# Another written-out order for the first long convolution and the front behind it

## The chip, the cores and the metric

The kernel runs on one core of one Trainium2 chip. The metric is the device time of one execution in microseconds (us). The engines are named as in the profile: TensorE (PE, with its weight loads as PEld), VectorE (DVE), ScalarE (ACT), GpSimd (POOL) and SyncE (SP), whose queue issues nearly all transfers.

## The reference

Four layers act on one sequence x of 2048 rows and 512 columns, each on a layer-normalized copy and with a residual sum: a local attention (A), a long convolution (B), and both again with the same weights.

```python
x = x + _A_ref(_layernorm(x), A_wqkv, A_wo)
x = x + _B_ref(_layernorm(x), B_A_re, ..., B_Dskip)
x = x + _A_ref(_layernorm(x), A_wqkv, A_wo)
x = x + _B_ref(_layernorm(x), B_A_re, ..., B_Dskip)
```

`_A_ref` has 32 heads of 16; each row attends to 8 rows at distances 0, 2, ..., 14 behind it. `_B_ref` makes a kernel K of 2048 taps for each column from the state-space parameters, and convolves each column with it by Fourier transforms of length 4096:

```python
Kf = rfft(pad(K)); Uf = rfft(pad(u))
y = irfft(Uf * Kf)[:L] + u * Dskip
```

## The kernel before

**Stages.** The program makes K, runs the first attention, then the first convolution, the second attention and the second convolution. The stage of this case is the first convolution (`FftB` with `tag` 0) with the *front* of the second attention behind it: layer norm, transposes and the projections to keys and queries.

**The convolution.** The transforms are matrix products in two steps. The columns are split into two groups of 256, and each kind of step below is done 16 times: numbers 0 to 7 are group 0, numbers 8 to 15 group 1. Each step is some matmuls into a result tile in PSUM, and a copy out of it (`evac`, L758, by ScalarE or VectorE) unless something else is said.

- `K`: first step of the transform of K (16 matmuls, L769, from `k_perm`).
- `U`: the same for the normalized input u, which lies in the tile `xnT`.
- `k`: second step for K (16 matmuls, L776). Its copy is a spectrum `kn`. It needs all eight `K` of its group.
- `u`: second step for u (L776). Its copy `ub` (L835) is always ScalarE's. It needs all eight `U` of its group. There are three `ub` buffers.
- `m`: the product. VectorE multiplies `ub` by `kn` and by `ks`, a copy of the spectrum with its rows swapped pairwise (two multiplies, L822), into the tile `t`.
- `y`: first inverse step (32 matmuls, L849), into `z`. It needs all eight `m` of its group. Group 0's `z` overwrites `xnT`.
- `z`: second inverse step, over four of the 16 row blocks; `z01` is group 0, rows 4 to 7. It needs all eight `y` of its group. With ScalarE, TensorE adds x (L873) and ScalarE copies the sum into `x_sb` (L880); with VectorE, VectorE adds (L878).

In what follows a letter with a number from 0 to 15 names a step (m15 is the last product); in the order strings the number is left out, because each kind is counted through.

**Transfers.** All of them are in SyncE's queue, in the order of the program. Behind a `k`, `kf_load` (L804) issues the two transfers of its swap `ks`, as soon as there is a buffer (`pump`, L794). Behind an `m`, `kf_dram` gets the spectrum for the second convolution (L825, the *store*), and the product's two buffers are free for later `k` and swaps. When all that is done, the queue goes on with the weights of the second attention (`front_w`, L244 and L245).

**Result tiles.** Four PSUM tiles are used in turn (`ptile`, L753), so a step waits for the copy four steps before it. The step `S` (`front_pools`, L1417) gives two of them to the front.

**The order.** `fb.run` (L882) reads one token after the other and issues the instructions of each. Inside `manual_schedule` each of TensorE, VectorE, ScalarE and SyncE works through its instructions in exactly that order. In a token a last `A` means ScalarE, `D` VectorE. `ORDER0` (L50) is the convolution, `ORDERF` (L56) goes on with it and mixes the front in. `LATE0` names small steps of the layer norm of u that are issued behind the first seven `K`; the first `U` waits for the normalized rows that one of them writes on GpSimd (L189).

**The front's tokens.** `h` row statistics of one group (four `bn_stats`, L142, VectorE), `a` their sum-up (L1424), `p` the reciprocal deviation (two small steps of ScalarE), `n` the normalized rows (L189, VectorE), `T` sixteen transposes into two PSUM tiles (L261), `E` the copy out of one of the two (L263), `P` a projection to keys (four matmuls, L272, copied by ScalarE, L275), `Q` one to queries (L215), `x` shifted copies of keys (L285). A first digit is the block of 512 rows, except in `h` and `z`, where it is the group, and in `Q`, where it is the block of queries.

```python
for tok in order.split():
    op, ix = tok[0], [int(c) for c in tok[1:] if c.isdigit()]
    eng = dict(A="act", D="dve", B="both").get(tok[-1])
    ...
    n = cnt[op] = cnt.get(op, -1) + 1
    g, t = divmod(n, 8)
```

Of the kernel before, what the change touches and what calls it, by code (L numbers as in the profile page):

```python
# [21 lines left out]
S = 2048  # L22
# [25 lines left out]
zktkKkUEETkeUUktKTkkUkKTUUeKkkpkxpKUxkpUEUxUKkqUxUUUUpqoUkpoxKXUQxoUkpkKXZpxXxpxZZ  # L48
"""
ORDER0 = """  # L50
KD KA KA KD KA KA KD KA KD KA KD kA kA KD kA KD UA UD UA UD UA kD UA UD UA KD
kA kD u kD kA u UA m KD m u u UD UA UA UA m UD u m KA UD u m u kA kD m kA UA
kD u kA m kA kD u m u kA m m u u yD yA u m yA u m m m u u m m
"""
LATE0 = "a s t g r b m"
ORDERF = """  # L56
yA yA yA yA yA yA yD yA yA yA z01D yD yA yA z00A z10A z11A h01 h00 h10 a0 z12A
p0 h11 z02A n0 a1 z03A h02 S T0 p1 E01D n1 E00A h12 a2 z13A P02 P01 h03 T1
E10A Q00 E11D p2 P03 P00 n2 h13 P10 P12 a3 T2 E21D E20A p3 n3 P11 P13 P23 P21
T3 E31D x1 E30A P20 P22  # L60
"""
ORDER1 = """
UD UA UD UA UD UA UD UA UD UA UD u UD u u m UA u m UD UA m u m u m
# [1440 lines left out]
```

## Time and profile before

| what | value |
|---|---|
| median of 3 runs (413.72 to 416.47) | 414.1 us |
| the profiled execution | 415.31 us, of which the span of instructions is 413.5 us |
| mean granted TensorE clock | 0.993 |
| TensorE busy | 323.4 us (78%) |
| VectorE busy | 382.7 us (93%) |
| ScalarE busy | 324.6 us (79%) |
| GpSimd busy | 37.3 us (9%) |
| first matmul of the convolution, first copy by VectorE | 193.28, 193.96 us |
| last product m15 ended | 242.55 us |
| first transposes of the front | 257.09 us |
| first product of the second attention (L332) | 275.72 us |

All times in the rows are microseconds from the start of the span. Shares are means over stages with different limits, so a stage is read by itself. In an answer, `[1.71 <-DMA w_sb<-kf_sb]` behind an instruction says that its engine stood idle for 1.71 us before it, and that this transfer ended the wait. `x4` is a run of four like instructions, with the time from the first's start to the last's end. The names of tiles can be those of the memory that they share: `w_sb`, `kn`, `kf_sb` and `kf_nat` are all spectra and swaps here.

### The profile page before, as it was taken

Reading aid. Unit: us, or ns where it says so; the run is one execution under the profiler, and the core shown is the slowest. Engines: PE = TensorE matmul, PEld = TensorE weight load, DVE = VectorE, ACT = ScalarE, POOL = GpSimd, SP = SyncE. Lnnn points to the kernel's source line nnn. Section 1 sums busy time; section 2 is a strip of 40 time slices with the busy share of each in tenths; the row PEclk is TensorE's granted clock in tenths of the full one; section 3 lists DMA queues with packets and bytes.
Section 4 is the critical chain, followed back from the end, with each engine's and each line's share of the span. In section 5 each row is a group of like instructions: output and inputs, shape, how many; then the busy total and the mean of one; then the engine's idle time right before and its main releaser. Section 6 shows DMA issues by size and latency. Waiting matters only on the chain.

```text
span 413.5 us, 15577 instructions
## 1 busy us (share of the span) xinstructions
PE 323.4 (78%) x6929; PEld 225.1 (54%) x6929; DVE 382.7 (93%) x500; ACT 324.6 (79%) x557; POOL 37.3 (9%) x48
## 2 busy tenths in 40 slices
PE   2000169899999988889998769999999979997775
PEld 2000126657756655556887658653466655566664
DVE  7999999999799999997999949979889999989985
ACT  5999999896445579997999988874566658889962
POOL 3000200000396000000400000000000020000000
PEclk9999999999999999999999989999999999999998
DMA  7930832123014756393235586750043018504507
GB/s 215 403 107 13 88 77 71 33 55 77 15 44 111 195 175 190 85 395 122 79 118 194 184 292 171 257 177 0 2 115 91 3 53 360 157 3 141 170 4 204
DMA packets 62325, 54.22 MB, mean 131 GB/s; under 512 B 33869, under 2 KB 50738, under 8 KB 60978
## 3 DMA queue, kind: packets, MB, share of 16 engines
q1 hardware_dynamic: 62250, 53.22, 42.0%
q8 instruction: 54, 0.88, 0.9%
q14 instruction: 13, 0.11, 0.1%
q10 hardware_dynamic: 8, 0.00, 0.0%
HBM read 30.15 MB, written 13.24 MB: 105 GB/s over the span
## 4 chain that ended last, share of the span: by engine, by line
PE 40%; DVE 21%; ACT 7%; DMA 6%; issue 5%; SPq 5%; DVEq 0%; ACTq 0%
DVE pav L457 7%; PE pq L388 6%; PE pk L1195 5%; PE pp L1133 4%; DVE a1s L758 4%; PE pq L215 3%; PE L L344 3%; DVE prod L332 3%; PE pp L272 3%; SPq L1300 2%; DMA w_sb<-w_dram 2%; PE po L472 2%; PE pb L849 2%; PE pq L483 2%; DVE t L822 2%
## 5 line engine op out<-in xcount | busy, mean ns | idle before, releaser
L457 DVE TENSOR_TENSOR pav<-attn,v_ext 128x4096 bf16<-128x4096 bf16 (+1 forms) x34 | 72.9, 2155 | 0.0
L332 DVE TENSOR_TENSOR prod<-qT,kT_ext 128x4096 bf16<-128x4096 bf16 x29 | 65.9, 2297 | 3.6 <-PE L L344 3.2
L472 PE MATMUL po<-ident,pav 64*128 64x64 bf16 x2048 | 36.0, 190 | 13.7 <-DVE pav L457 7.9
L472 PEld LDWEIGHTS <-pav 64*128 64x128 bf16 x2048 | 32.4, 95 | 24.8 <-DVE pav L457 17.1
L1123 PE MATMUL pt<-ident,x_blk 128*128 128x128 bf16 x64 | 6.3, 241 | 42.2 <-DMA w_dram<-w_q 40.7
L1037 DVE TENSOR_TENSOR A_t<-A_t,pow_t 128x1024 bf16<-128x1024 bf16 (+4 forms) x46 | 38.0, 868 | 0.2
L835 ACT CAST ub<-pb 128x1024 bf16<-128x1024 f32 x32 | 32.1, 1042 | 1.2 <-ACT a1s L758 0.3
L776 PE MATMUL pb<-a1s,w_sb 128*128 128x64 bf16 x768 | 27.5, 193 | 6.9 <-ACT a1s L758 2.6
L483 PE MATMUL pq<-wop,oT 128*128 128x512 bf16 x128 | 32.8, 379 | 0.0
L390 ACT CAST v_ext<-pq 128x512 bf16<-128x512 f32 x32 | 18.8, 587 | 17.0 <-PE pq L388 15.7
L1133 PE MATMUL pp<-xnT,kT_ext 128*128 128x512 bf16 x96 | 26.8, 407 | 5.4 <-ACT qT L1138 2.5
L388 PE MATMUL pq<-wv,xnT 128*128 128x512 bf16 x128 | 30.8, 379 | 0.0
L758 DVE CAST a1s<-pb 128x1024 bf16<-128x1024 f32 x23 | 27.0, 1214 | 3.4 <-PE pb L769 3.4
L776 PEld LDWEIGHTS <-w_sb 128*128 128x128 bf16 x768 | 25.0, 98 | 9.4 <-issue 7.5
L1123 PEld LDWEIGHTS <-x_blk 128*128 128x128 bf16 x64 | 4.8, 107 | 44.6 <-ACT x_blk L187 43.2
L758 ACT CAST a1s<-pb 128x1024 bf16<-128x1024 f32 x25 | 24.9, 1037 | 2.2 <-PE pb L769 1.9
L474 ACT CAST oT<-po 128x512 bf16<-128x512 f32 x32 | 18.5, 578 | 9.7 <-PE po L472 9.5
L849 PE MATMUL pb<-Wp,t 64*128 64x64 bf16 x512 | 19.6, 195 | 6.4 <-ACT ub L835 1.8
L849 PEld LDWEIGHTS <-t 64*128 64x128 bf16 x1024 | 17.8, 98 | 11.2 <-issue 6.3
L1195 PEld LDWEIGHTS <-A_t 128*64 128x64 bf16 (+1 forms) x512 | 21.8, 103 | 3.7 <-issue 0.2
L1195 PE MATMUL pk<-B_t,A_t 128*64 128x84 bf16 (+1 forms) x512 | 23.6, 201 | 0.0
L215 PE MATMUL pq<-xnT,kT_ext 128*128 128x512 bf16 x96 | 23.5, 379 | 0.0
(241 smaller groups left out, 823.1 us busy)
## 6 DMA issues: line engine op xcount, KB each, us to landing
w_sb<-w_dram SPq DMA_DIRECT2D x8, 1024.0 KB, 7.1
w_dram<-xnT SPq DMA_DIRECT2D x1, 4096.0 KB
kf_ring<-kf_dram SPq DMA_DIRECT2D x13, 256.0 KB, 4.5
kf_ring<-kf_dram SPq DMA_DIRECT2D x26, 128.0 KB, 3.7
v_ext<-v_ext SPq DMA_DIRECT2D x4, 784.0 KB, 6.1
x_blk<-in_A_x_dram SPq DMA_DIRECT2D x4, 512.0 KB, 4.0
kT_ext<-in_A_wqkv_dram SPq DMA_DIRECT2D x4, 512.0 KB, 9.5
x_sb<-in_A_x_dram SPq DMA_DIRECT2D x4, 512.0 KB, 5.7
```

Source lines behind the costliest of these rows:

```text
L215: nc.tensor.matmul(pq[:], lhsT=self.wqk[:, dt, ft * P:(ft + 1) * P], rhs=self.xnT[:, dt, q * 512:(q + 1) * 512], start=(dt == 0), stop=(dt ...
L332: nc.vector.tensor_tensor(pr, self.qT[q][:, ft].unsqueeze(1).to_broadcast([P, W, 4, P]), kap, ALU.mult)
L388: nc.tensor.matmul(pp[:], lhsT=xnT[:, dt, a * P:(a + 1) * P], rhs=wv[:, dt, :], start=(dt == 0), stop=(dt == NDT - 1))
L457: nc.vector.tensor_tensor(pv[:, i], attn[:, n % 4].unsqueeze(2).to_broadcast([P, W, DH // parts, H]), vap, ALU.mult)
L472: nc.tensor.matmul(po[:, h, 0, i * nt + ft, :], lhsT=pvf[rows, i, w, ft * P:(ft + 1) * P], rhs=ident[rows, rows], start=(w == 0 and ft + i ...
L483: nc.tensor.matmul(pw[:], lhsT=oT[:, ftp, :], rhs=self.wo[:, ftp, :], start=False, stop=(ftp == NDT - 1))
L758: (self.nc.scalar.copy if eng == "act" else self.nc.vector.tensor_copy)(dst, src)
L776: nc.tensor.matmul(p2[:, j, :], lhsT=self.w2[:, ec * EC + j, :], rhs=a1s[:, ec * EC + j, :], start=True, stop=True)
L849: nc.tensor.matmul(p3[:, h, j, :], lhsT=tt[rows, dql, :], rhs=w[rows].rearrange("p m d -> p (m d)"), start=first, stop=not first)
L1037: return lambda: nc.vector.tensor_tensor(*args)
L1133: nc.tensor.matmul(pps[kind, b, ft][:], lhsT=la.wqk[:, dt, c:c + P], rhs=la.xnT[:, dt, b * 512:(b + 1) * 512], start=(dt == 0), stop=(dt = ...
L1195: nc.tensor.matmul(o, lhsT=lhs, rhs=Bt[:, ri, c * CH + ql].rearrange("p b g -> p (b g)"), start=(not half and j % 4 == 0 and ri == 0), sto ...
```

## The change

Two order strings are replaced. Each kind of step occurs as often as before, and nothing else is edited. Some copies go to the other engine: in the convolution VectorE has eight `K` instead of nine, five `U` instead of six, seven `k` instead of six and five `y` instead of three; in the front E20 and E30 go from ScalarE to VectorE.

```diff
 ORDER0 = """
-KD KA KA KD KA KA KD KA KD KA KD kA kA KD kA KD UA UD UA UD UA kD UA UD UA KD
-kA kD u kD kA u UA m KD m u u UD UA UA UA m UD u m KA UD u m u kA kD m kA UA
-kD u kA m kA kD u m u kA m m u u yD yA u m yA u m m m u u m m
+KD KA KA KA KA KD KD KA KA KD kA kD kA KD KA KD UA kD UA UA UD UA UD UA KD UA kA kD kA u kD UA u UA m KD m u UD m u UA u m KA u UD kA UA m UD kD m kA UA u u m u kD u kA kD kA u kA m u u u m m m u m m yA m yD yA u yA yA m m yA yD yA yD yA yD yA z01D yA
 """
 LATE0 = "a s t g r b m"
 ORDERF = """
-yA yA yA yA yA yA yD yA yA yA z01D yD yA yA z00A z10A z11A h01 h00 h10 a0 z12A
-p0 h11 z02A n0 a1 z03A h02 S T0 p1 E01D n1 E00A h12 a2 z13A P02 P01 h03 T1
-E10A Q00 E11D p2 P03 P00 n2 h13 P10 P12 a3 T2 E21D E20A p3 n3 P11 P13 P23 P21
-T3 E31D x1 E30A P20 P22
+yA yA yD z00A h01 z10A h00 z11A S z12A h10 a0 p0 h11 n0 z02A h02 a1 z03A T0 E00A E01D p1 z13A n1 h12 a2 P01 P02 T1 E10A E11D Q00 h03 P03 p2 n2 P12 P00 h13 P11 T2 a3 P10 E20D E21D p3 P13 P21 P23 n3 T3 x1 E30D P22 E31D P20
 """
```

With the numbers written in, the stretch around the last products is, before:

```
u10 u11 y0D y1A u12 m10 y2A u13 m11 m12 m13 u14 u15 m14 m15 | y3A y4A y5A y6A y7A y8A y9D ...
```

and after:

```
u10 k15A m7 u11 u12 u13 m8 m9 m10 u14 m11 m12 y0A m13 y1D y2A u15 y3A y4A m14 m15 y5A y6D y7A y8D ...
```

In SyncE's queue the store behind m7 now comes after the swap of k15 instead of before it.

## Prediction

> **What bounds the kernel now.** I read the page for the shares of the engines first, then the change's two stretches as windows, then the chain of waits, and last the timelines of VectorE, ScalarE and SyncE's queue there. The windows below are the first convolution up to its last product, from there to the first transpose of the second front, the rest of the front, and everything behind it.
>
> ```profile
> 193.30:242.60 49.30, 40.74 (x1283) 36.40 (x1282) 46.19 (x62) 47.59 (x53) 6.04 (x8) 1.00 0.45 162
> 242.60:258.40 15.80, 15.66 (x350) 13.78 (x351) 11.56 (x34) 12.31 (x16) 0.35 (x1) 0.89 0.74 224
> 258.40:274.70 16.30, 16.30 (x121) 9.48 (x119) 13.43 (x45) 12.86 (x24) 0.00 (x0) 1.00 0.78 269
> 274.70:413.50 138.80, 119.45 (x2725) 78.99 (x2723) 127.30 (x111) 96.78 (x169) 2.89 (x1) 0.99 0.31 98
> ```
>
> Columns are length, then busy time of TensorE, its weight loads, VectorE, ScalarE and GpSimd, then the granted clock, the DMA share and GB/s. Up to 242.6 the two evacuating engines have no room: VectorE is busy 46.2 of 49.3 us, ScalarE 47.6. From 242.6 TensorE sets the pace, at a mean clock of 0.89, and in the front at full clock without a gap. The change edits only these three rows; the fourth should follow as a block.
>
> The chain of waits shows where one row turns into the next:
>
> ```profile
> 234.90 1.70 SPq L804
> 236.65 0.58 SPq L825
> 237.84 3.93 DMA w_sb<-kf_sb
> 241.86 0.70 DVE t L822
> 242.61 3.65 PE pb L849 x158
> ```
>
> The last product m15 waits for the swapped copy of its spectrum (L804). That transfer is issued late because SyncE's queue is full, and lands at 241.8. VectorE and TensorE stand still meanwhile:
>
> ```profile
> 239.47 0.68 DVE L822 TENSOR_TENSOR t<-ub,kf_sb 128x1024 bf16<-128x1024 bf16 x1
> 241.86 0.69 DVE L822 TENSOR_TENSOR t<-ub,w_sb 128x1024 bf16<-128x1024 bf16 x1 [1.71 <-DMA w_sb<-kf_sb]
> 243.73 1.22 DVE L758 CAST z<-pb 128x1024 bf16<-128x1024 f32 x1 [1.18 <-PE pb L849]
> 247.63 1.23 DVE L878 TENSOR_TENSOR x_sb<-pb,x_sb 128x1024 bf16<-128x1024 f32 x1 [2.68 <-PE pb L875]
> ```
>
> And a second loss follows the first. TensorE has next to nothing to do from 239.6 to 242.6, and from 243.5 to 247 its clock is halved, just where it sets the pace:
>
> ```profile
> 240.00:241.00 1.00, 0.20 (x2) 0.10 (x2) 0.15 (x1) 1.00 (x2) 0.00 (x0) 1.00 0.32 109
> 241.00:242.00 1.00, 0.00 (x0) 0.00 (x0) 0.14 (x1) 1.00 (x2) 0.00 (x0) 1.00 0.65 242
> 243.00:244.00 1.00, 1.00 (x68) 1.00 (x62) 0.27 (x1) 0.74 (x1) 0.35 (x1) 0.78 1.04 389
> 245.00:246.00 1.00, 1.00 (x46) 1.00 (x42) 0.00 (x0) 1.00 (x2) 0.00 (x0) 0.50 1.04 367
> 247.00:248.00 1.00, 1.00 (x38) 0.77 (x37) 0.37 (x1) 0.43 (x1) 0.00 (x0) 1.00 0.93 324
> ```
>
> A clock of 0.89 over 15.8 us is 15.8 x 0.11 = 1.74 us lost.
>
> **Prices.** These are start-to-start costs in full queues:
>
> ```profile
> 201.46 4.63 DVE L758 CAST a1s<-pb 128x1024 bf16<-128x1024 f32 x4 [0.16 <-PE pb L769]
> 194.41 3.76 ACT L758 CAST a1s<-pb 128x1024 bf16<-128x1024 f32 x4 [0.43 <-PE pb L769]
> 233.36 4.99 DVE L822 TENSOR_TENSOR t<-ub,kf_nat 128x1024 bf16<-128x1024 bf16 x8
> 212.99 1.10 SPq L804 DMA_DIRECT2D w_sb<-kn  x2
> 237.33 1.11 SPq L804 DMA_DIRECT2D w_sb<-kf_sb  x2
> 237.15 1.01 ACT L835 CAST ub<-pb 128x1024 bf16<-128x1024 f32 x1 [0.19 <-DVE t L822]
> ```
>
> A copy costs VectorE (4.63 - 1.21) / 3 = 1.14 us and ScalarE (3.76 - 1.02) / 3 = 0.91. A product is two multiplies of (4.99 - 0.68) / 7 = 0.61, so 1.2. SyncE issues 31 transfers between 212.99 and 238.44, 0.82 us each with all its pauses.
>
> **Part 1, the first convolution up to m15.** No instruction is added or removed; copies change engine and place. Before, VectorE's queue up to m15 holds 22 copies (9 K, 6 U, 6 k, 1 y) and 16 products: 22 x 1.14 + 32 x 0.60 + 1.9 for the small statistics = 46.2, plus idle 0.16, 0.52 and 1.71 = 48.6, which is 193.96 to 242.55. After, it holds 21 (8 K, 5 U, 7 k, 1 y): 45.05. Walking through both queues by hand with the prices above I find 0.85 us of small waits (k1, k7 and K12 behind TensorE), so m15 could end at 239.9.
>
> Two others must allow that. ScalarE has 36 copies from U0 (203.05 in both orders, since U0 waits for GpSimd's rows at 202.2) to the copy u15. Its pace before over that kind of stretch was (237.15 - 203.05) / 35 = 0.97, so u15 starts at 238.1, ends at 239.0 and m15 at 240.2. In that pace lies one new wait: the u copies have three buffers, and the new order writes u10 to u13 ahead of m8, so the copy u10 must stand behind m7, u11 behind m8, u12 behind m9, u13 behind m10. Queued behind the standing u10 on ScalarE is k15, whose swap m15 needs. I place m7's end at 229.2 and k15's end at 231.0; SyncE only gets to that swap at 235, so 4 us cover it.
>
> SyncE: swap 4 waits for store 0 to land and for m0. k3 stands after one U instead of five, so store 0 goes out some 2 us earlier, and m0 becomes the later one; swap 4 is issued at 212.25 instead of 212.99. From there to swap 15 there are 30 transfers instead of 31, because store 7 falls behind it: 212.25 + 30 x 0.82 = 236.9, landing 3.4 us later as before, 240.25, and m15 ends at 240.85. Nine stores instead of eight now follow swap 15 in the queue, and behind them the loads of the second layer's weights: 236.9 + 9 x 0.8 = 244.1, against 244.49 before. Landing 6 us later they are there by 250.5, and nothing needs them before 255.
>
> The three answers are 239.9, 240.2 and 240.85. I take **240.5, which is -2.05**; its ends are 239.9 and, if the swap is no earlier than now, 242.5.
>
> **Part 2, from m15 to the end of the first transposes (T0).** TensorE's list is eight y, one z by VectorE, six z by ScalarE and T0: 8 x 0.50 + 0.86 + 6 x 1.31 + 0.89 = 13.6 at full clock. It took 242.61 to 258.43 = 15.8: 1.74 for the clock, 0.45 in T0, which waits row by row for the normalized rows n0. After, only y5 to y7 (1.5 us of TensorE) lie between u15 and m15, but y3 and y4 are copied earlier and the pause before y8 shrinks from 2.2 us to 1.4 or less, so I expect **no halved clock**. T0 still waits about 0.35 for n0. 13.6 + 0.35 = 13.95, **-1.85**. VectorE is nearly level here: five copies, four statistics of 1.3, a0 and n0 are 5.7 + 5.2 + 1.9 = 12.8 us, so 1.1 us of cover; beyond that each of its waits counts. The step S, which takes half of the result buffers away, now comes before z12. Two are left for z12, z02 and z03; a ScalarE copy (1.01) is shorter than the 1.31 of the next z, so it costs nothing while ScalarE keeps up.
>
> **Part 3, the front.** In VectorE's new queue the second T0 copy (E01) is behind n0, h02 and a1. With n0 done at 254.0, h02 and a1 take 1.65, E01 0.6: 256.25, while TensorE is through z13 at 255.8. **+0.5.** E20 and E30 move from ScalarE (1.0 each) to VectorE (0.6 each). VectorE's list from there is 15 us against TensorE's 17 to the last projection, so this costs nothing; without that cover, 1.2.
>
> **Sum:** -2.05 - 1.85 + 0.5 = -3.4 on a span of 413.5. The profiled execution took 415.3 and the median shown is 414.1 (three runs, 413.7 to 416.5), so the profile stands 1.2 above it and I apply the difference: 414.1 - 3.4 = **410.7**. Its own range is 409.2 to 412.
>
> [...]
>
> **Rivals.**
> (a) *The clock halves all the same.* The new order packs m7 to m13 with little for TensorE to do, about half of its time from 229 to 237, against 0.6 to 0.7 before. Then the 1.74 stays: 414.1 - 2.05 - 0.1 + 0.5 = 412.4. For it: a pause of 2.2 us was enough here. [...] 0.15.
> (b) *Slower: SyncE's queue sets the end.* Swaps 10 to 15 are issued at its pace, and the products now want them 0.8 to 1.8 us earlier than before. Some single issues took 1.5 to 2.0 us instead of 0.56. If the pace is 0.95 instead of 0.82, swap 15 lands at 212.25 + 28.5 + 3.4 = 244.2, m15 ends at 244.8 (+2.25), TensorE has been idle since y7 for some 5 us, the clock halves (-0.1 in place of -1.85), E01 adds 0.5: 416.7. It decides from a landing at 241.6 on (0.865 a transfer): there the three terms cancel. Against it: one transfer fewer and an earlier start. 0.12.
> (c) *VectorE becomes the bound of the front.* With two more copies there and 0.3 us for each hop to ScalarE's small steps p1 to p3, its 15 us grow to over 17: 1.2 us given back, 411.9. For it: it was busy with one gap of 0.3 us from 249.9 to 268.5. 0.08.
> (d) *More gain:* m15 at 239.9, no wait at E01: 414.1 - 2.65 - 2.0 = 409.4. 0.15.
> The order does do what it says, since each engine runs its list as written.
>
> **Chances and range.** Forecast 0.50, (a) 0.15, (b) 0.12, (c) 0.08, (d) 0.15. What a measurement of this kernel can tell from no change is about 1%, that is 410.0 and 418.2. (d) mostly and a third of the forecast lie below 410.0: 0.31. Above 418.2 lies only the far end of (b): 0.07. Range 408.8 to 415.6: it takes in (a), (c), (d) and the near half of (b).
>
> **What would show it.** Right: m15's second multiply without a wait above 0.7 us and ended by 241; granted clock 1.00 from 240 to 256; T0 ended near 254.5; the first product of the second attention (L332, 275.7 now) at 272 to 273; ScalarE's u10 with a wait of about 0.8 on VectorE's products. Wrong: a DMA wait before m12 to m15, a clock row at 0.5 behind 238, or TensorE waiting for E21 or E31 in the front.

## The result, and the profile after

The changed kernel took 418.47 us (median of 9 runs, 416.62 to 420.98) against 414.46 us (413.38 to 417.37) for the kernel before beside it: a ratio of **1.0081**, 95% interval 1.0052 to 1.0109. Forecast were 410.7 us and a range that ends at 415.6. Two later measurements of the same changed kernel gave 1.0003 (0.9979 to 1.0028) and 1.0027 (1.0002 to 1.0052), with medians of 415.95 and 416.72 us against 415.60 and 415.47 for the kernel before. So the new order is not faster anywhere, and slower by something between nothing and 1%.

The profiled execution took 416.79 us, one of the fastest of the nine; its span is 415.0. These are the windows of after that answer to the four of before (up to m15, to the end of T0, the rest of the front, everything behind), with the same columns:

```profile
194.50:241.60 47.10, 40.15 (x1283) 36.62 (x1282) 45.39 (x62) 45.65 (x52) 6.05 (x8) 1.00 0.46 169
241.60:259.10 17.50, 14.53 (x350) 12.65 (x351) 13.71 (x33) 12.85 (x16) 0.35 (x1) 1.00 0.66 205
259.10:275.50 16.40, 16.40 (x121) 9.47 (x119) 14.72 (x50) 11.16 (x22) 0.00 (x0) 1.00 0.75 252
275.50:415.00 139.50, 121.83 (x2725) 80.65 (x2723) 127.51 (x111) 96.48 (x169) 2.89 (x1) 0.97 0.31 99
```

The first row is shorter than before's by 2.2 us, where 2.05 were forecast. The second is *longer* by 1.7, although its clock is now 1.00 as forecast: TensorE is busy for 14.5 of 17.5 us where it was busy throughout. The timeline of TensorE shows where it stands in that row:

```profile
243.97 0.20 PE L844 MATMUL pb<-WpJ,t 64*128 64x64 bf16 x1 [1.01 <-issue]
248.79 0.20 PE L844 MATMUL pb<-WpJ,t 64*128 64x64 bf16 x1 [1.79 <-issue]
```

"issue" means that TensorE waited for nothing that the profile shows: no copy, no transfer, no product. Both waits lie in the middle of a step (y10 and y13), where all operands are there. The chain of waits shows how the second reaches T0, because y15's copy is VectorE's and twelve statistics, n0 and T0 stand behind it:

```profile
247.00 1.79 issue
248.79 1.21 PE pb L844 x69
250.02 1.23 DVE z L753
251.25 3.95 DVE ln_bn L137 x12
...
256.95 1.40 DVE xn L184 x4
258.39 0.90 PE pt L256 x13
```

Landmarks of all profiles in us: K0 is the first copy of the convolution, T0 the start of the first transposes, "product" the first of the second attention (L332, now L327). Waits are those for nothing shown, on TensorE between m15 and T0.

| kernel | K0 | K0 to m15 | m15 to T0 | T0 to product | waits |
|---|---|---|---|---|---|
| before | 193.96 | 48.59 | 14.54 | 18.63 | none |
| before again (e5) | 194.45 | 46.09 | 14.56 | 18.64 | none |
| after | 195.17 | 46.38 | 16.24 | 18.74 | 2.8 |
| after again (e4) | 194.39 | 46.38 | 15.36 | 18.73 | 1.9 |
| after, third (e11) | 197.53 | 46.40 | 16.27 | 18.75 | 1.3, and half clock |
| e1, new order up to m15 only | 195.24 | 46.38 | 17.46 | 18.63 | 3.4 |
| e2, new order from m15 only | 195.50 | 46.47 | 13.71 | 18.73 | 0.4 |
| e3, after with held weights | 195.23 | 46.37 | 14.57 | 18.73 | 1.1 |
| e6, after with shifted blocks | 196.77 | 46.37 | 20.49 | 18.74 | 4.6 |
| e7, after with few transfers | 196.04 | 46.37 | 14.05 | 18.74 | 0.7 |
| e8, e2 with held weights | 196.09 | 46.29 | 14.08 | 18.74 | 0.8 |
| e9, even mix | 194.34 | 46.80 | 16.94 | 19.10 | 0.5 |
| e10, e9 with held weights | 195.36 | 46.40 | 17.64 | 19.10 | 1.3 |

In the stretch from m15 to T0 the granted clock fell to 0.50 in before, e5, e6 and e11; in the other profiles it stayed at 1.00.

The pair of profiles adds up: K0 later by 1.21, then -2.21, +1.70, +0.11, +1.04 from the first product to the second convolution (90.46 to 91.50) and -0.35 behind it, +1.5 in all. The first and the last two stretches hold the same instructions in both kernels.

### The profile page after: what moved, and what is told of

Same layout as the page of the kernel before. It is cut to its first block, busy times and chain, and to the rows that moved or that the text cites. A ratio compares the mean times of both kernels' runs of the same rounds, so it can differ in the third digit from the quotient of the medians.

```text
span 415.0 us, 15579 instructions
## 1 busy us (share of the span) xinstructions
PE 324.5 (78%) x6929; PEld 226.1 (54%) x6929; DVE 385.8 (93%) x503; ACT 321.2 (77%) x554; POOL 37.3 (9%) x48
## 4 chain that ended last, share of the span: by engine, by line
PE 40%; DVE 21%; ACT 10%; issue 7%; DMA 4%; SPq 2%; DVEq 0%; ACTq 0%
PE pq L383 6%; DVE pav L452 6%; PE pk L1190 5%; PE pp L1128 4%; DVE t L817 3%; PE pq L210 3%; PE L L339 3%; DVE a1s L753 3%; PE pp L267 3%; DMA v_ext<-v_ext 3%; PE po L467 3%; PE pq L478 2%; DVE prod L327 2%; DVE t L814 2%; SPq L1295 2%
## 5 line engine op out<-in xcount | busy, mean ns | idle before, releaser
L327 DVE TENSOR_TENSOR prod<-qT,kT_ext 128x4096 bf16<-128x4096 bf16 x29 | 65.9, 2299 | 3.6 <-PE L L339 3.2
L771 PE MATMUL pb<-a1s,w_sb 128*128 128x64 bf16 x768 | 29.0, 197 | 7.3 <-ACT a1s L753 4.3
L478 PE MATMUL pq<-wop,oT 128*128 128x512 bf16 x128 | 33.7, 387 | 0.0
L771 PEld LDWEIGHTS <-w_sb 128*128 128x128 bf16 x768 | 26.5, 100 | 9.7 <-issue 7.3
L753 ACT CAST a1s<-pb 128x1024 bf16<-128x1024 f32 x27 | 26.9, 1038 | 2.1 <-PE pb L764 1.9
L753 DVE CAST a1s<-pb 128x1024 bf16<-128x1024 f32 x21 | 24.7, 1216 | 3.7 <-PE pb L764 3.7
L339 PEld LDWEIGHTS <-prod 128*128 128x128 bf16 x672 | 19.6, 96 | 6.2 <-DVE prod L327 1.9
L844 PE MATMUL pb<-Wp,t 64*128 64x64 bf16 x512 | 18.6, 190 | 5.2 <-issue 1.3
```

What stands on the lines that cost most here:

```text
L327: nc.vector.tensor_tensor(pr, self.qT[q][:, ft].unsqueeze(1).to_broadcast([P, W, 4, P]), kap, ALU.mult)
L478: nc.tensor.matmul(pw[:], lhsT=oT[:, ftp, :], rhs=self.wo[:, ftp, :], start=False, stop=(ftp == NDT - 1))
L753: (self.nc.scalar.copy if eng == "act" else self.nc.vector.tensor_copy)(dst, src)
L771: nc.tensor.matmul(p2[:, j, :], lhsT=self.w2[:, ec * EC + j, :], rhs=a1s[:, ec * EC + j, :], start=True, stop=True)
```

## Experiments 1 and 2: each half of the change alone

e1 has the new order up to m15 and the old tail and front; e2 the reverse.

```diff
 e1:  ORDER0 = "KD KA KA KA KA KD ... u yA yA m m"          (as after, up to m15)
      ORDERF = "yA yA yA yA yD yA yA yA z01D yD yA yA z00A z10A ..."   (as before)
 e2:  ORDER0 = as before
      ORDERF = "yA yA yA yD yA yD yA yD yA z01D yA yA yA yD z00A h01 z10A h00 z11A S ..."
```

> The new order up to the last product m15, the old one behind it (y5 to y7 by ScalarE, old front). Theory F (TensorE's instructions, in blocks of 256, come late while the transfers saturate the DMA engines from 239 to 249): m15 ends some 2 us earlier than before, the clock stays at 1.00, but two waits of 1 to 2 us on nothing shown (issue) stand 128 weight loads apart behind y8, as in the changed kernel; time within 1.5 us of the changed kernel, slower than before. Rival T (the new tail and front cost the time, E copies on VectorE, S early): with the old tail the gain of m15 stays, 2 to 3 us faster than before.

> The old order up to m15, the new tail and front behind it. Theory F: m15 waits 1.7 us for its swap and the clock halves as before, which hides the late instructions; time within 1 us of before. Rival T: slower than before by what the changed kernel loses, 3 us.

Measured: e1 1.0009 (0.9981 to 1.0036), e2 1.0000 (0.9971 to 1.0029). Neither half moves the time; theory F had expected e1 to be slower than before. In the profiles e1 has the short first stretch and a longer second one than the changed kernel (17.46, with waits of 1.05 and 2.3 us for nothing shown). e2 has the *old* order up to m15 and still takes 46.47 there, so that the short stretch is no mark of the new order. Neither the late swap nor the half clock that were expected of e2 came: at full clock, with only 0.4 us of waits for nothing, it went from m15 to T0 in 13.71 us.

## Experiments 3 and 4: the weights held, and the changed kernel again

Two things stand beside the waits for nothing: the transfer engines are full (share 0.73 to 1.08 around both in after), by the nine stores and the weights of the second attention (two transfers of 512 KB). e3 keeps the weights back until z01 is done, by a transfer of 128 bytes that reads z01's result and stands ahead of them in SyncE's queue.

```diff
-    la.front_w()
...
+        def weights():
+            nc.sync.dma_start(scr[:], x_sb[0:1, 4, 0:64])
+            la.front_w()
...
-yA yA yD z00A h01 ...
+w yA yA yD z00A h01 ...
```

> The changed kernel with the weights of the second attention (two loads of 512 KB) held in SyncE's queue until z01 is done, by a transfer of 64 numbers that reads its rows. Theory F: the second wait on issue, near 247 to 249, goes or shrinks under 0.5 us, the first (near 243) stays, since the nine stores cause that; 1.5 to 2 us faster than the changed kernel. Rival T, and rival C (the time is lost to the clock in later stages, not here): no difference over 0.5 us.

> The changed kernel once more, for a second profile. Theory F: the same two waits on issue behind y8, 2.5 to 3 us together, at the same instructions. What lies ahead of 193 us and behind 277 us is the same code in both kernels; if the 1.2 us by which it was later at 194 us is chance it differs here, if it comes from the code it stays.

Measured: e3 1.0013 (0.9982 to 1.0044), e4 1.0003 (0.9979 to 1.0028). On the weight loads, the wait in y13 is 1.36 us in e4 and 0.54 in e3; the wait in y10 stays (0.80 and 0.83): there the weights are not yet issued, and only stores are under way. With the weights held the second wait is shorter (experiment 12 shows why), but the 1.5 to 2 us that were expected of the whole time did not come. In the profiles the two differ by 0.8 us in this stretch, less than the same code differs between executions elsewhere.

## Experiment 5: the kernel before again

> The kernel before, one more execution, for the stretch lengths. Theory R (the 1.71 us wait for the last swap and the halved clock behind it belong to this order): first K copy to the end of m15 again 48.3 to 48.9 us, m15 to T0 again 14.3 to 14.8, a wait of 1.5 us or more before m15's second multiply. Theory C (they were one execution's): 46.3 to 47.0 for the first stretch, as the old order up to m15 took in e2 (46.47), with the wait before m15 below 0.7.

Measured: 46.09 us to m15, without a wait for a swap. Theory C: the 1.71 us were one execution's. Of four profiles with the old order up to m15 (before, e2, e5, e8) one has them. But the clock halves all the same. The timelines of VectorE and TensorE, then the windows, of e5:

```profile
239.26 0.68 DVE L822 TENSOR_TENSOR t<-ub,kf_sb 128x1024 bf16<-128x1024 bf16 x1
239.86 0.68 DVE L822 TENSOR_TENSOR t<-ub,w_sb 128x1024 bf16<-128x1024 bf16 x1
```

```profile
238.11 0.21 PE L849 MATMUL pb<-Wp,t 64*128 64x64 bf16 x2 [0.50 <-ACT ub L835]
240.60 0.20 PE L849 MATMUL pb<-WpJ,t 64*128 64x64 bf16 x2 [0.40 <-DVE t L822]
```

```profile
239.00:240.00 1.00, 0.64 (x32) 0.52 (x33) 1.00 (x3) 1.00 (x2) 0.00 (x0) 1.00 0.41 152
240.00:241.00 1.00, 0.60 (x28) 0.49 (x30) 0.54 (x1) 1.00 (x2) 0.00 (x0) 0.97 0.14 43
241.00:242.00 1.00, 1.00 (x48) 1.00 (x42) 0.00 (x0) 1.00 (x2) 0.00 (x0) 0.50 1.02 381
243.00:244.00 1.00, 1.00 (x46) 1.00 (x42) 0.46 (x1) 1.00 (x2) 0.00 (x0) 0.50 1.06 381
```

TensorE's longest pause in the six us ahead is 0.50, it is busy for 0.60 to 0.68 of each microsecond, and then runs at half clock for 3.4 us. The prediction had put the half clock down to the pause of 2.2 us; no such pause is needed. At half clock the y come more slowly (in before every 0.83 to 0.85 us from 243.52 to 245.21, against every 0.46 to 0.48 at full clock), and no wait for nothing appears.

## Experiment 6: do the waits count instructions?

In the profiles with two such waits they stand 128 weight loads apart, which with their matmuls are 256 TensorE instructions. The page of after lists a queue of kind "instruction": 54 packets, 0.88 MB, which is 16 KB a packet, or 64 bytes for each of TensorE's 13,858 instructions. Theory F: TensorE's instructions come in blocks of 256 over the same engines as the data, and TensorE stands at a block's border when the next is late. If so, 64 matmuls more, anywhere earlier, move every border by 64 loads.

```diff
+        extra = pst.tile([P, 4, P], F32, name="pt")
+        for _ in range(64):
+            nc.tensor.matmul(extra[:, 0, 0:64], lhsT=ident[:], rhs=ident[:, 0:64], start=True, stop=True)
```

> The changed kernel with 64 matmuls of 64 columns more, while TensorE is idle early in the program; their result is read by nobody. Nothing else is changed. Theory F (TensorE stands until its next 256 instructions, that is 128 weight loads and 128 matmuls, have been fetched by a queue that shares the transfer engines): the two long waits for nothing, until now 2 loads into y10 and 26 loads into y13, move 64 loads forward, to 2 loads into y8 and into z01, and one may come late in y15; none is left over 0.3 us inside y10 and y13. Rival G (the waits belong to the steps or to what VectorE and ScalarE do then): they stay inside y10 and y13, 0.8 to 1.9 us each. Time: within 1.5 us of the changed kernel by either.

Measured (timeline of TensorE, and windows):

```profile
244.20 0.20 PE L844 MATMUL pb<-WpJ,t 64*128 64x64 bf16 x1 [0.80 <-issue]
250.39 0.39 PE L870 MATMUL pb<-xnT,g_sb 128*128 128x256 bf16 x1 [3.75 <-issue]
```

```profile
249.00:250.00 1.00, 0.00 (x0) 0.00 (x0) 0.00 (x0) 0.00 (x0) 0.00 (x0) 0.83 0.08 15
251.00:252.00 1.00, 1.00 (x21) 0.58 (x21) 0.32 (x1) 0.00 (x0) 0.00 (x0) 0.50 0.07 22
```

The waits moved to exactly the foreseen places, 2 loads into y8 and 2 loads into z01, and none is left in y10 and y13. Rival G falls. The size was not foreseen: at z01 TensorE stood for 3.75 us, meanwhile its clock went to half (0.83 in 249 to 250, 0.50 up to 256), and m15 to T0 took 20.49 us; this single execution took 422.16, 3.7 more than the changed kernel's slower median. So with 64 idle matmuls, 230 us earlier, this stretch took 4 to 5 us more than in the three profiles of after.

## Experiment 7: hardly any transfers

```diff
-        if self.tag == 0:
+        if self.tag == 0 and g == 0:
             self.nc.sync.dma_start(self.kf_dram[g, ec]...)
...
+        for ec in range(NEC):
+            nc.sync.dma_start(kf_dram[1, ec]..., x_sb[:, 2 * ec:2 * ec + 2, :]...)
```

with the weights held as in e3.

> The changed kernel with the transfers between m8 and z01 taken away: the stores of group 1's spectra are replaced by eight transfers of the same size from x_sb, issued before the convolution (so the second convolution works on other data for group 1), and the weights of the second attention are held behind z01. Theory F: without those bytes TensorE's next instructions come in time: no wait over 0.4 us inside y10 and y13, m15 to T0 in 13.6 to 14.0 us instead of 15.4 to 16.2, and the whole time 1 to 2.5 us below the changed kernel's 416, that is 413.5 to 415, a ratio of 0.994 to 0.999 to the kernel before. Rival G: 15.4 or more, and a ratio of 1.000 or above.

Measured: 1.0030 (1.0004 to 1.0055), m15 to T0 14.05 us. The stretch came out near what theory F gave (13.6 to 14.0), the whole time did not: a miss. And one wait is left where no transfer of data is under way (the wait by the timeline, and the last columns of the windows, the DMA share and GB/s):

```profile
247.46 0.20 PE L845 MATMUL pb<-WpJ,t 64*128 64x64 bf16 x1 [0.70 <-issue]
```

```profile
243.00:244.00 1.00, 0.94 (x59) 0.83 (x54) 1.00 (x2) 1.00 (x3) 0.00 (x0) 1.00 0.00 0
244.00:245.00 1.00, 1.00 (x58) 0.93 (x51) 1.00 (x2) 1.00 (x3) 0.00 (x0) 1.00 0.08 16
246.00:247.00 1.00, 0.77 (x53) 0.65 (x45) 1.00 (x1) 0.60 (x1) 0.00 (x0) 1.00 0.00 0
```

What moves in the second row, 16 GB/s for one microsecond, is 16 KB: one block of instructions, and the DMA share counts it with 0.08. So theory F in the form "transfers make the blocks late" says too little. Even alone the block took 3.73 us from border to border here, longer than TensorE needs for four y in a row (4 x 0.47 = 1.9 us, at 0.46 to 0.48 each in after); beside full transfer engines it was 4.28 to 6.20 (the table of experiment 12). The trace of *before* had it already, in the second convolution's y steps, with a DMA share of 0.00 around it:

```profile
398.82 0.20 PE L849 MATMUL pb<-Wp,t 64*128 64x64 bf16 x2 [1.08 <-issue]
```

## Experiments 8, 9 and 10: orders that should suffer less

e8 is e2 with the weights held. e9 puts group 0's second inverse steps between group 1's y, and one more y copy on VectorE; e10 is e9 with the weights held.

```diff
-... m m yA yD yA yD yA yD yA z01D yA | yA yA yD z00A h01 z10A h00 z11A S z12A h10 a0 p0 h11 n0 z02A h02 a1 z03A T0 ...
+... m m yA yD yA yD yA z01D yD yA z00A | h01 yD yA z02A h00 yA yD z10A h02 z11A S z12A h10 a0 p0 h11 n0 z03A a1 T0 ...
```

> The old order up to m15, the new order from there (as e2), and the weights held behind z01 (as e3). Theory F: e2's one wait of 0.52 us goes, m15 to T0 in 13.2 to 13.7; the weights still land before the first projection, so T0 to the first product stays 18.6 to 18.8; ratio 0.997 to 1.000. Rival: the held weights land too late and the first projections wait 1 us or more: the front takes 19.7 or more, and the ratio is above 1.002.

> The changed kernel with its tail in another order: group 0's second inverse steps stand between group 1's first ones instead of behind them (y5 to y9, z01, y10, y11, z00, y12, y13, z02, y14, y15, z10, z11, z12, z03, T0, z13), so that TensorE never has more than five y in a row behind m15; one more y copy is VectorE's. The same steps, matmuls and transfers. Theory F (a y step uses up 64 TensorE instructions in 0.5 us, and 256 of them need some 3.5 us to come, more beside many transfers): the z spread out the need, the waits for nothing fall from 2.8 (1.9 in e4) to 1.0 us or less in sum, m15 to T0 in 14.0 to 15.0 us instead of 15.4 to 16.2, ratio to before 0.995 to 1.000. Rival G (the copies or the transfers set this stretch): 15.4 or more, ratio 1.000 to 1.008.

> As e9, and the weights of the second attention are held behind z01. Theory F: fewest waits of all versions, 0.5 us or less in sum; m15 to T0 13.6 to 14.2; T0 to the first product unchanged at 18.6 to 18.8; ratio 0.993 to 0.999. Rival: the sparse hold makes the first projection wait for its weights, T0 to the first product 19.5 or more, ratio 1.000 or above.

Measured: e8 1.0020 (0.9990 to 1.0049), e9 1.0081 (1.0052 to 1.0110), e10 1.0076 (1.0051 to 1.0101). Theory F had expected a ratio of 1.000 or less of each, so these are misses; e10 also had 1.3 us of waits and 17.64 us from m15 to T0, against 0.5 or less and 13.6 to 14.2. In e8 the held weights did not free the border (0.89 us on the weight loads instead of e2's 0.52), and the front did not wait. In e9 the waits for nothing fell as theory F said, to 0.5 us in sum, and the stretch still took 16.94 where 14.0 to 15.0 were expected: another wait took their place.

```profile
250.70 1.23 DVE L753 CAST z<-pb 128x1024 bf16<-128x1024 f32 x1 [0.26 <-PE pb L844]
...
254.44 1.41 DVE L137 BATCH_NORM_STATS2 ln_bn<-x_sb 128x6 f32<-128x256 bf16 x4 [1.20 <-ACT x_sb L875]
```

```profile
251.98 0.28 PE L869 MATMUL pb<-z,g_sb 128*128 128x256 bf16 x1 [1.11 <-DVE z L753]
```

With z00 and z02 moved ahead, nothing stands between y15 and z10: z10 waits 1.11 us for y15's copy (first row), and VectorE 1.20 us for z10's copy (second row) before it can go on to h10 and n0, for which T0 waits. T0 to the product grew as well, by 0.4. The reordering gave back on this chain what it saved in instructions; no version run here beats the kernel before. Where the waits stand theory F foretold, what the whole execution takes it did not.

## Experiment 11: the changed kernel a third time

> The changed kernel once more, to tell its size against before: the first measurement gave 1.0081, e4 1.0003. If the true difference is that of the waits (two executions: 1.5 us more and 2.4 us less than before's profile), the ratio is 1.000 to 1.005; if the first measurement was right, 1.006 or more. K0 to m15 46.4 again, and waits of 0.8 us or more in y10 and y13.

Measured: 1.0027 (1.0002 to 1.0052). In its profile the first border's wait is 1.32 us, and now the clock halves behind it: 0.88 in 246 to 247, 0.50 up to 250, 0.91 in the next, some 1.7 us lost. The half clock is not bound to the old order.

## Experiment 12: the supply of instructions by itself

1024 very short matmuls early in the program, where TensorE has nothing else to do and waits for no data (the granted clock there is 0.50).

```diff
+        extra = [pst.tile([P, 4, P], F32, name="pt") for _ in range(2)]
+        for i in range(1024):
+            h = slice(64 * (i % 2), 64 * (i % 2) + 64)
+            nc.tensor.matmul(extra[i % 2][:, 0, 0:16], lhsT=ident[h, :], rhs=ident[h, 0:16], start=True, stop=True)
```

> The changed kernel with 1024 small matmuls more (weights of 64 rows and 128 columns, 16 columns each, into two tiles that nobody reads), early in the program, from some 11 us on, where TensorE waits for nothing and has nothing else to do until 48 us. Transfers fill the engines until about 22 us and are few behind that. Theory F: TensorE runs them in groups of 128 loads with a wait at each border; from border to border 3.2 to 3.8 us where the transfers are few, 4.5 us or more where they are many, however short the matmuls are. Rival G (the tail's waits come from something else, and TensorE's instructions come as fast as it can take them): no border shows, and the 1024 run through at 16 to 35 ns each, 128 in 2 to 4.5 us by the clock alone, evenly. The whole time is of no interest (it can be up to 6 us more).

The timeline of TensorE:

```profile
18.76 1.88 PE L1002 MATMUL pt<-ident 64*128 64x16 bf16 x128 [4.20 <-issue]
24.95 1.88 PE L1002 MATMUL pt<-ident 64*128 64x16 bf16 x128 [4.32 <-issue]
28.68 1.88 PE L1002 MATMUL pt<-ident 64*128 64x16 bf16 x128 [1.85 <-issue]
32.69 1.88 PE L1002 MATMUL pt<-ident 64*128 64x16 bf16 x128 [2.12 <-issue]
36.69 1.88 PE L1002 MATMUL pt<-ident 64*128 64x16 bf16 x128 [2.13 <-issue]
40.42 1.88 PE L1002 MATMUL pt<-ident 64*128 64x16 bf16 x128 [1.85 <-issue]
```

```profile
18.00:20.00 2.00, 1.24 (x93) 1.24 (x94) 2.00 (x4) 2.00 (x3) 0.00 (x0) 0.50 1.01 384
```

Groups of exactly 128, each run through in 1.9 us, with a wait at every border. From border to border: 28.68 to 32.69 and so on, **3.73 to 4.01 us** where the transfers are few, and 6.19 (18.76 to 24.95), most of it, up to some 23 us, beside full engines (share 1.01, 384 GB/s). The page's instruction queue grew from 54 to 62 packets, one for each 128 loads added. Expected were 3.2 to 3.8 and 4.5 or more. Theory F stands in its second form: here TensorE gets 256 instructions in some 3.7 to 4.0 us when alone and in 6.2 beside full transfer engines, with 16 columns (3.73 to 4.01 and 6.19 in e12) or with 64 (3.73 in e7, 6.20 in e6).

The traces also date each packet of the instruction queue, and with them the waits fall into three pieces. Times are in us, borders are taken on the weight loads, and the share is that of the transfer engines from the last border to the packet's start:

| wait ended | packet starts, behind the last border | share | packet takes | TensorE goes on, behind the packet's end | border to border |
|---|---|---|---|---|---|
| e7, 247.46 | 1.13 | 0.00 | 1.27 | 1.33 | 3.73 |
| e12, 28.68 | 1.12 | 0.07 | 1.18 | 1.42 | 3.73 |
| after, 243.96 | 1.89 | 1.06 | 0.96 | 1.43 | 4.28 |
| after, 248.79 | 2.56 | 1.02 | 0.95 | 1.32 | 4.82 |
| e6, 250.39 | 3.95 | 0.95 | 0.97 | 1.28 | 6.20 |

Every wait of the table ends 1.3 to 1.4 us behind the end of a packet, so it is these packets that TensorE stands for. Beside full engines they start later (1.9 to 3.95 us behind the border instead of 1.1) and take no longer (0.95 to 0.97 us against 1.18 and 1.27); that made e6's wait so long, and with the weights held the packet of e3's second wait started 1.13 behind the border, against 2.10 in e4.

## Why the prediction was wrong, point by point

**Part 1 (forecast -2.05).** Its walk through the queues was good: K0 to m15 fell by 2.21 in the pair, u10 waited 0.50 us on m7's product where 0.8 was foreseen (first row), and swap 15 was in time, since m15's second multiply did not wait (second row):

```profile
230.90 1.01 ACT L830 CAST ub<-pb 128x1024 bf16<-128x1024 f32 x1 [0.50 <-DVE t L817]
240.87 0.68 DVE L817 TENSOR_TENSOR t<-ub,w_sb 128x1024 bf16<-128x1024 bf16 x1
```

The new order was forecast to be at m15 46.5 us behind K0 and took 46.4. The step that failed is the base: 1.71 us of the 48.6 were a swap's lateness in one execution, and were counted as this order's. The old order takes 46.09 to 46.47 without it, the new one 46.37 to 46.40. The term is about 0, and the pair's -2.21 agrees with the forecast only because before's profile was that execution: luck. Whether the new order keeps the swap from being late at all stays open.

**Part 2 (forecast -1.85).** "No halved clock" came true in the pair (1.00 from 240 to 256). The failed step is "TensorE's list ... 13.6 at full clock": y steps were priced at 0.50 each, eight and more in a row, as if instructions came without limit. From y5 on the new order has 11 y and z01 in a row, 360 weight loads or 2.8 blocks: by estimate, at the 3.7 to 4.0 us a block of e12, 10 to 11 us of supply for 6.4 us of matmuls at the forecast's prices; the waits measured are 2.8 us. The half clock of before had hidden this: it stretches four y from 1.9 to 3.4 us (4 x 0.84), not far from a block's 3.7 to 4.0 (in e5 TensorE crossed the border at 245.90 without standing, 1.3 us behind the packet's end, as close as in the waits). Taking it away turned 1.74 us of slow matmuls into 2.8 us of waiting; the term measured +1.7 in the pair. The 1.1 us of cover given for VectorE was right in kind: the waits of 2.8 us exceeded it and went on to T0. Part of the gain was there to be had: in e2, at full clock and with 0.4 us of such waits, the stretch took 13.71, which is 0.8 less than before.

**Part 3 (forecast +0.5).** +0.1. In after, E01 did stand behind h02 and a1 and ended at 260.53, but TensorE was in z13 until 260.61, so it held nobody up. E20 and E30 cost nothing, as foreseen.

**The rivals.** (a) is half right: the clock can halve in the new order (e11), behind a wait for instructions of 1.32 us. The pause of 2.2 us that (a) builds on is not needed: in e5 pauses of 0.50 us at most, with TensorE busy for 0.60 to 0.68 of each microsecond, end in half clock. From 231 to 240 in before, pauses of 0.27 to 0.57 us had gone with a clock of 1.00. (b), the slow one, was not what happened: SyncE issued swap 15 early enough. (c) and (d) did not occur. The cause that did was in no rival.

**What stays open.** The edited stages (K0 to the product) average 81.1 us in three profiles of after and 80.5 in two of before: 0.6 us, or 0.14%; the two of before differ by 2.5 between themselves. That fits the second and third measurement, not the first with 0.8%. Same code swings by more: K0 lies between 193.96 and 197.53, and the stretch from the first product to the second convolution between 90.46 and 92.46. Why the first measurement showed 4 us was not settled. Of the three profiles of after only e11's is as much slower than before's, by 4.6 us, and 3.6 of these lie ahead of K0, where both kernels are the same.

## What to carry to other kernels

Before a loss is booked as a gain, ask what it covers: a stretch at half clock, or a late transfer, may stand in front of another bound, and one profile's wait may not be the order's. For stages of many small matmuls count the instructions as well as the time: here such waits ended 3.5 (e3) to 6.2 us (e6) behind the border before, where four y use a block up in 1.9, and they read "issue", in the middle of a step, 128 weight loads apart. In e6 64 matmuls added earlier moved them by 64 loads, and with the same steps the stretch took 4 to 5 us more.

## What the runs showed that was not expected

- In e12 TensorE's instructions arrived in blocks of 256, 3.7 to 4.0 us apart where the transfers were few and 6.2 beside transfers of 384 GB/s. In the table of experiment 12 a waiting TensorE goes on 1.3 to 1.4 us behind the end of the packet. With matmuls of 64 columns TensorE uses a block up in 1.9 us (4 x 0.47, from the y of after).
- 64 matmuls added 230 us earlier moved both waits by 64 loads and one of them was then 3.75 us.
- The clock went to 0.50 with TensorE busy for 0.60 of the time and no pause above 0.50 us (e5), and did not in the new order with 0.49 to 0.73 from 232 to 239 (after). In the traces of before and after its changes lie whole multiples of 3.41 us apart (in before down at 243.55, up at 246.96, down at 410.80; in after at 342.74, 346.15, 383.70, 387.11 and 414.42); by the windows the half clock lasted 3.4 us in e5 and e11 and 6.8 in e6. In the 3.41 us ahead of the fall TensorE was busy for 0.39 (e6), 1.15 (before), 1.72 (e11) and 1.90 us (e5); behind 1.79 (after, 247.17 to 250.58) the clock stayed at 1.00. So no single pause is needed, and what exactly decides is not settled here.
